# A planned attention and convolution kernel: new cost constants for the order, and 108 instead of 95 pairs of score tiles on VectorE

## The chip, the cores and the metric

The kernel runs on one core of a Trainium2 chip. A core has five engines that run side by side, each through its own instructions in a fixed order: TensorE (PE, matmuls; its weight loads are shown apart as PEld), VectorE (DVE), ScalarE (ACT), GpSimd (POOL) and SyncE (SP, which here only issues DMAs). They wait for each other through semaphores. SBUF is the on-chip memory with 128 partitions. PSUM is the memory that matmuls write, in eight banks of 512 float32 columns. The metric is the device time of a run in microseconds (us), and the median of the runs is compared.

## The reference

The inputs are a sequence x of 2048 tokens with 640 features, and k and v of the same shape. Two branches are computed and mixed by a gate for each token:

```python
x = A_q
g = _sigmoid((x * gate_w).sum(-1, keepdims=True))
a = _A_ref(x, A_k, A_v, A_shift_k, A_ssm_k, A_ssm_D)   # long convolution
b = _B_ref(x, B_wq, B_wk, B_wv, B_wo)                  # attention
return g * a + (1 - g) * b
```

Branch A shifts k with a four-tap filter, multiplies by v, convolves each feature over the sequence with ssm_k through a Fourier transform of length 4096, adds `kv * ssm_D` and multiplies by x. Branch B is attention with 32 heads of 20 features that share one key and one value head:

```python
scores = jnp.einsum("bhqd,bkd->bhqk", q, k) * (Dh ** -0.5)
p = _softmax(scores, axis=-1)
o = jnp.einsum("bhqk,bkd->bhqd", p, v)
```

There is no mask, so every head has 2048 x 2048 scores, 134 million exponentials in all.

## The kernel before

**Attention.** A score tile is 128 keys by 512 queries of one head, one PSUM bank. Four heads form a group and sit in four groups of 32 rows of TensorE's array, so that their matmuls (K = 20) can run at once. There are 32 groups G (four blocks I of 512 queries, eight groups each), with 16 key chunks j in each. The last group (LASTG = 31) is cut into three stages of 256, 128 and 128 queries, which makes its last work short. `stream` lists the tiles in order and packs them into units of three and of two tiles by turns. `QK` (L1210) writes the scores of a unit into PSUM banks 0 to 2 or 3 to 4. `EXP` (L1247) is one ScalarE instruction for a unit, from PSUM into a buffer ETA (three tiles) or ETB (two tiles); there are NET = 3 of each. `PV` (L1288) multiplies by the values with a column of ones, which gives the sum of the exponentials too, and accumulates over the 16 chunks in bank 6. The keys hold an offset that keeps the exponentials in range.

**Pairs on VectorE.** For the chunks that DVE_J names for a group, two of the four heads' tiles are left out of the stream. `DEXP` computes their exponential on VectorE: two reads of PSUM (dW, L1277, 512 wide) that scale the score into the bits of a 16-bit number, then three steps of a polynomial in the lower bits, 1024 wide (dX L1280, dX L1281, ETd L1283). There are NED = 4 buffers ETd, two dW and one dX. Their scores go to bank 5 or 7 and "ride" in row groups that a unit leaves free. Their PV matmuls use `vneg`, may only run after the first PV of the group, and must be done before its last.

**Side work.** The same engines do, between the exponentials: the query projections of the next block (L1115, L1126, sq L1130), the shift of k (L1514), the Fourier matmuls in five blocks c of 128 features and eight frequency blocks (`spectra`, L1571, with VectorE copies X L1584 and K L1590, L1592), the complex products on GpSimd (`mac`, L1604: three products of 512, one sum of 512, two of 256), the inverse transforms (`inverse`, L1637, L1647), the normalisation (`norm`: a copy of the accumulator L1356, a reciprocal, DMAs through DRAM that spread it over partitions as rbc, a GpSimd product L1368), and the output projections (`oproj` L1667 and L1670, `part` L1393 and L1396, `tail` L1423, L1447 and L1478). Side work has the PSUM banks 7 and 5 (SIDE).

**The order.** Nothing is reordered on the chip. A planner in the kernel's own source (`Scheduler`) walks through a simulated time and writes each engine's order once. Every operation has a cost (c_ps, c_fast, c_pool, c_mm, c_exp: a constant and a slope in columns) and a priority. Between engines it adds a latency (LATM, LATX). SBUF's second port, which VectorE and GpSimd share, is modelled by two times: port_until and pool_until, with the offsets PORTP and PORTD. A VectorE operation marked `port=True` starts when the last GpSimd one is done, and a GpSimd operation when the last such VectorE one is done. `pick_work` chooses for TensorE: the next operation of the main queue (score and PV matmuls in program order) when it can start, otherwise side work that fits the gap. `pick` takes the candidate of the best priority for the other engines. `emit` writes the instructions with waits on semaphores. Where TensorE would be idle, dummy matmuls (L1719) are put in. The constants change the planned order, never how long an instruction takes.

Of the kernel before, what the change touches and what calls it, by code (L numbers as in the profile page):

```python
# [23 lines left out]
LATM = {("dve", "dve"): 0.3, ("pool", "pool"): 0.0}  # L24
# [24 lines left out]
class Op:  # L49
    __slots__ = ("eng", "fn", "deps", "cost", "kind", "name", "prio", "grp", "alts", "port", "nbytes", "main",  # L50
                 "cont", "nun", "succ", "ready", "start", "end", "placed", "sig", "value", "lane", "known", "seq",
                 "banks", "last", "urge", "floating", "tail", "attached", "lat", "iss", "row", "soft", "cols", "hole", "unit")

    def __init__(self, eng, fn, cost, kind, name, prio):
        self.unit = None
        self.eng = eng
# [113 lines left out]
class Scheduler:  # L170
# [34 lines left out]
    def run(self):  # L205
# [6 lines left out]
        self.main_q = {"pe": [o for o in g.all if o.main and o.eng == "pe"],  # L212
                       "act": [o for o in g.all if o.main and o.eng == "act"]}
        self.main_pos = {"pe": 0, "act": 0}
# [43 lines left out]
    def pick(self, e, t):  # L258
# [12 lines left out]
        if e == "pool" and self.main_started and not self.pool_may(t):  # L271
            return None
        for o in self.cand[e]:
            if o.ready <= t:
# [3 lines left out]
                k = (o.prio, o.seq)  # L278
# [50 lines left out]

    def pick_work(self, t):  # L330
        q = self.main_q["pe"]
        p = self.main_pos["pe"]
        m = q[p] if p < len(q) else None
# [38 lines left out]
        if m is not None:  # L372
            if m.cont:
                if m.nun == 0:
                    self.main_pos["pe"] += 1
                    return m
                return None
            if m.nun == 0:
# [7 lines left out]
                if ok:  # L386
                    if r <= t:
                        self.main_pos["pe"] += 1
                        return m
# [60 lines left out]
    def place(self, op, e):  # L450
# [54 lines left out]
        if op.name in ("tp0", "tp1"):  # L505
# [4 lines left out]
            self.filler = self.filler2.pop(0) if self.filler2 else None  # L510
        if op.name == "pv":
            self.can_fill = not op.last
# [123 lines left out]
PORTP = 0.145  # L636
PORTD = 0.04
LASTG = 31
STAGES = ((0, 256, 6), (256, 128, 5), (384, 128, 6))
DVE_J = ((), (), (1, 6, 11), (4, 11), (2, 6, 10, 14), (4, 9, 14), (3, 8, 13), (3, 8, 11), (2, 6, 10, 14), (4, 9, 14), (1, 5, 8, 13), (2, 7, 12), (3, 8, 13), (2, 5, 8, 11, 14), (5, 12), (1, 5, 9, 13), (4, 9, 14), (4, 9, 14), (4, 9, 14), (1, 4, 8, 12), (2, 6, 10, 14), (3, 8, 13), (2, 4, 13), (1, 7, 13), (1, 6, 11), (1, 6, 11), (1, 4, 11), (3, 9), (1, 4, 7, 10, 13), (2, 5, 8, 11, 14), (2, 9), ())  # L640
MAC_ALT = ()
# [7 lines left out]
def c_fast(n):  # L649
    return 0.16 + 0.52e-3 * n  # L650

# [17 lines left out]
class Kernel:  # L669
# [256 lines left out]
    def tables2(self):  # L926
# [11 lines left out]
        for name in ("Tsin", "Tcos"):  # L938
# [7 lines left out]
            for c in range(1, H):  # L946
                self.evac(gr, "dve", lambda e, bk, name=name, c=c: e.tensor_copy(
                    T[name][:, c, 0:128 * c], self.bank_bf(bk, 128 * c, 64 * c * (c - 1))), (), [(name, c)],
                    c_fast(128 * c))
# [157 lines left out]
    def qproj(self, I, gs, prio, banks, ng):  # L1107
# [4 lines left out]
        for gl, gi in enumerate(gs):  # L1112
            gr = self.group("qp", prio, banks=banks)
            for dc in range(NDC):
# [4 lines left out]
                if dc == 0:  # L1119

                    o.deps.update(self.crow0 or ())
                    if self.crow0:
# [4 lines left out]
                          qt[:, gi, :], self.bank(bk), T["qup"][:, 0:1], None, ALU.add)), c_ps(512) + 0.055),  # L1127
# [4 lines left out]
                     [(f"qT{par}", gi)], [("sq", gl)], c_fast(512), prio=-1500.0 if I == 0 and gs[0] < 3 else prio - 500, port=True,  # L1132
# [646 lines left out]
```

## Time and profile before

| What | Before |
|---|---|
| Median of three runs | 868.13 us (867.65 to 868.68) |
| Span of the profiled execution | 865.2 us |
| Own time of the profiled execution | not listed; the median is 2.9 us above its span |
| Granted TensorE clock | 1.000 |
| First / last start of an exponential (L1247) | 19.55 / 858.17 us |
| VectorE busy in 19.5 to 125, 125 to 225, 525 to 625 us | 84.43, 88.22, 87.59 us |
| VectorE busy in 800 to 858.2 us | 25.67 us |
| Dummy matmuls L1719 in the stream | 73.84 us |

The page gives for each engine its busy time, its share of the span and its instructions. The chain is the work that ended last, followed back from the end. A group row reads: line, engine, operation, output<-input, shapes, count | busy us, mean ns of one | idle time before it, and who ended that. A timeline row reads: start, duration (a merged row: of all), engine, line, operation. A row of waits reads: engine and line waiting <- who ended it: us in total, times, longest. A row by stretch reads: stretch, its length, then busy us (and instructions) of PE, PEld, DVE, ACT, POOL, the clock, the DMA share, GB/s. Records of neighbouring instructions on ScalarE and VectorE overlap, so the distance of starts is the cost of one, not its duration.

### The profile page before, as it was taken

What the parts mean: (1) busy time and instruction counts of PE and PEld (TensorE: products, weight loads), DVE (VectorE), ACT (ScalarE), POOL (GpSimd) and SP (SyncE); (2) the same over time, 40 slices, a digit from 0 to 9 for tenths busy, and PEclk for the clock granted to TensorE, in tenths of its full rate; (3) what the DMA queues carried; (4) which work ended last, traced back from release to release, by engine and by line L of the source; (5) the groups of instructions that cost most, each with busy time, mean ns of one, the idle gap of its engine ahead of it and who ended that gap; (6) DMA issues with size and microseconds to landing.
All of it is one profiled execution on the core that took longest, in us unless ns stands there. A gap on an engine that the chain in (4) does not pass through costs nothing.

```text
span 865.2 us, 18881 instructions
## 1 busy us (share of the span) xinstructions
PE 842.1 (97%) x8139; PEld 350.5 (41%) x8159; DVE 710.2 (82%) x923; ACT 852.8 (99%) x764; POOL 389.8 (45%) x355
## 2 busy tenths in 40 slices
PE   8999999999999999999999999999999999999997
PEld 5234433344334434444434333444443444333444
DVE  8588888898999898979898988988888776688434
ACT  6999999999999999999999999999999999999997
POOL 4582000448655353665544662417677437630000
PEclk9999999999999999999999999999999999999999
DMA  7800020000100000020000021000020000041210
GB/s 197 211 14 9 20 45 20 21 14 8 44 21 20 14 20 8 20 45 20 20 15 9 19 44 49 30 14 8 20 45 20 15 14 3 13 103 39 75 60 32
DMA packets 49729, 30.71 MB, mean 35 GB/s; under 512 B 32493, under 2 KB 45678, under 8 KB 49646
## 3 DMA queue, kind: packets, MB, share of 16 engines
q1 hardware_dynamic: 49070, 29.29, 12.5%
q8 instruction: 63, 1.03, 0.5%
q10 hardware_dynamic: 576, 0.22, 0.1%
q14 instruction: 20, 0.16, 0.1%
HBM read 17.85 MB, written 6.02 MB: 28 GB/s over the span
## 4 chain that ended last, share of the span: by engine, by line
ACT 97%; PE 2%; DVE 0%; issue 0%; POOL 0%; POOLq 0%
ACT ETA L1247 58%; ACT ETB L1247 39%; PE ps L1724 1%; PE ps L1019 0%; PE ps L1051 0%; ACT xT L726 0%; PE ps L1115 0%; DVE outsb L1478 0%; DVE tprod L912 0%; POOL iota_f L865 0%; PE ps L1210 0%; PE ps L1423 0%; PE ps L1288 0%; DVE ident L873 0%; DVE acc L1409 0%
## 5 line engine op out<-in xcount | busy, mean ns | idle before, releaser
L1247 ACT ACTIVATE ETA<-ps 128x1536 bf16<-128x1536 f32 x372 | 607.2, 1632 | 0.2 <-PE ps L1210 0.2
L1247 ACT ACTIVATE ETB<-ps 128x1024 bf16<-128x1024 f32 x371 | 449.5, 1212 | 0.0
L1210 PE MATMUL ps<-qT,kT 32*128 32x512 bf16 (+2 forms) x2176 | 297.9, 371 | 12.9 <-ACT ETA L1247 7.6
L1604 POOL TENSOR_TENSOR Pp<-X,K 128x512 f32<-128x512 bf16 x120 | 164.7, 1390 | 156.5 <-DVE dX L1281 58.0
L1210 PEld LDWEIGHTS ps<-qT,kT 32*128 32x128 bf16 x2176 | 75.7, 91 | 242.2 <-ACT ETB L1247 124.2
L1277 DVE TENSOR_SCALAR dW<-ps 128x512 f32<-128x512 f32 x190 | 130.2, 685 | 42.6 <-PE ps L1210 40.7
L1288 PE MATMUL ps<-ETA,vaug 128*32 128x512 bf16 (+2 forms) x1195 | 153.1, 370 | 0.3 <-ACT ETB L1247 0.3
L1288 PE MATMUL ps<-ETB,vaug 128*32 128x512 bf16 (+2 forms) x791 | 149.7, 371 | 0.7 <-ACT ETA L1247 0.7
L1283 DVE SCALAR_TENSOR_TENSOR ETd<-dX,dW 128x1024 int16<-128x1024 f32 x95 | 134.2, 1413 | 15.4 <-PE ps L1288 15.2
L1281 DVE SCALAR_TENSOR_TENSOR dX<-dX,dW 128x1024 f32<-128x1024 f32 x95 | 133.6, 1407 | 0.2
L1280 DVE SCALAR_TENSOR_TENSOR dX<-dW 128x1024 f32<-128x1024 uint16 x95 | 131.5, 1385 | 0.9
L1604 POOL TENSOR_TENSOR AB<-Pp 128x256 bf16<-128x256 f32 x80 | 73.4, 917 | 57.7 <-DVE dX L1280 21.3
L1571 PE MATMUL ps<-ssm_kT,Tcs 128*128 128x256 bf16 x600 | 89.5, 274 | 0.0
L1637 PE MATMUL ps<-AB,Tcs 128*128 128x256 bf16 x600 | 88.4, 274 | 0.0
L1571 PE MATMUL ps<-kv,Tcs 128*128 128x256 bf16 x600 | 87.5, 275 | 0.1
L1368 POOL TENSOR_TENSOR oTn<-acc,rbc 128x512 bf16<-128x512 f32 x24 | 41.2, 1716 | 84.4 <-DMA rbc<-scr_d 37.7
L1719 PE MATMUL ps<-Tcs,zeros 128*32 128x512 bf16 (+1 forms) x920 | 74.2, 379 | 0.9 <-DVE acc L1356 0.7
L1604 POOL TENSOR_TENSOR Pp<-Pp 128x512 f32<-128x512 f32 x40 | 52.7, 1317 | 34.9 <-DVE dX L1281 10.8
L1637 PEld LDWEIGHTS ps<-AB,Tcs 128*128 128x128 bf16 x600 | 51.7, 98 | 32.6 <-issue 26.4
L1571 PEld LDWEIGHTS ps<-ssm_kT,Tcs 128*128 128x128 bf16 x600 | 50.6, 97 | 33.2 <-issue 26.3
L1571 PEld LDWEIGHTS ps<-kv,Tcs 128*128 128x128 bf16 x600 | 49.5, 98 | 35.5 <-issue 26.1
L1368 POOL TENSOR_TENSOR oT<-acc,rbc 128x512 bf16<-128x512 f32 x7 | 10.7, 1524 | 80.0 <-DMA rbc<-scr_d 47.8
(135 smaller groups left out, 645.4 us busy)
## 6 DMA issues: line engine op xcount, KB each, us to landing
rbc<-scr_d SPq DMA_DIRECT2D x31, 256.0 KB
scr_o<-oTn SPq DMA_DIRECT2D x24, 128.0 KB, 1.7
kv<-in_A_v_dram SPq DMA_DIRECT2D x4, 640.0 KB, 4.7
out_dram<-outsb SPq DMA_DIRECT2D x15, 160.0 KB, 1.9
xn<-in_A_q_dram SPq DMA_DIRECT2D x3, 640.0 KB, 6.9
oTp<-scr_o SPq DMA_DIRECT2D x12, 160.0 KB, 3.1
wog<-in_B_wo_dram SPq DMA_DIRECT2D x4, 200.0 KB
wo<-in_B_wo_dram SPq DMA_DIRECT2D x4, 200.0 KB
```

The source lines that it names most:

```text
L1210: return e.matmul(self.bank(bk, n, n * t), T["kT4"][32 * r:32 * r + 32, 128 * jt:128 * jt + 128], T[k][32 * r:32 * r + 32, g, q0:q0 + n], ...
L1247: op("act", lambda e: e.activation(et(n)[:, 0:w], self.ps[:, lo:lo + w], ACT.Exp, scale=SCALE), [("ps", base[n % 2] + k) for k in range(le ...
L1277: self.evac(gr, "dve", lambda e, bk, h=h: e.tensor_scalar(W[:, 512 * h:512 * h + 512], self.bank(bk), SCALE * LOG2E * 128.0, 128.0 * (127 ...
L1280: V(lambda e: e.scalar_tensor_tensor(X[:, :], w, DP, w, ALU.add, ALU.mult), [kW], ["dX"], c_ps(1024), **k)
L1281: V(lambda e: e.scalar_tensor_tensor(X[:, :], X[:, :], DQ, w, ALU.add, ALU.mult), [kW], ["dX"], c_ps(1024), **k)
L1283: V(lambda e: e.scalar_tensor_tensor(T[f"ETd{pe}"][:, :].bitcast(dt.int16), X[:, :], DA, W[:, :], ALU.mult, ALU.add), [kW, "dX"], [("ETd", ...
L1288: return op("pe", lambda e: e.matmul(self.bank(b, n)[32 * r:32 * r + 32, :], T[va][:, j, :], src, start=(j == 0), stop=(j == NSC - 1), til ...
L1368: self.pool(lambda e: e.tensor_tensor(out, T["acc"][:, :], T["rbc"][:, :], ALU.mult), ["acc", "rbc"], [key], c_pool(512), prio=p, port=Tru ...
L1571: self.mm(gr, lambda e, bk, lhs=lhs, rhs=rhs, comp=comp, n=n: e.matmul(self.bank(bk, 256, 256 * comp), lhs, rhs, start=(n == 0), stop=(n = ...
L1604: f = lambda e: e.tensor_tensor(out, a, b, alu)
L1637: self.mm(gr, lambda e, bk, lhs=lhs, fc=fc, comp=comp, h=h: e.matmul(self.bank(bk, 256, 256 * h), lhs, AB[:, fc, :, comp, :], start=(fc == ...
L1719: sch.filler, *sch.filler2 = ([[lambda e, r=r, st=st, b=b, n=n: e.matmul(self.bank(b, n)[32 * r:32 * r + 32, :], self.T["zeros"][:, 0:32], ...
```

## The change

- **Planner constants.** LATM gets times for each pair of engines: 0.127 between dependent VectorE operations (was 0.3), and 0.135, 0.06, 0.13 and 0.08 where 0.12 stood for all others. PORTP and PORTD change. VectorE's cost becomes c_dve and c_dve2 for the work in the stream.
- **Two main queues.** Score matmuls and PV matmuls get a queue each. `head` takes them in program order, except that scores go first when they can start and the PV batch cannot. Late PV matmuls are tied to the group's last PV batch whichever matmul of it comes first.
- **VectorE's choice.** While GpSimd is busy for over PORTW = 0.2 more, operations without the shared port go first.
- **DVE_J.** 108 pairs instead of 95, in groups 1 to 31 instead of 2 to 30, in other chunks. In group 31 a pair covers two halves of 256 queries in its first stage. A branch for steps in PSUM (INB) is there, but INB is empty.
- **mac.** The products of both parts of X with the first part of K become one of 1024; five GpSimd operations instead of six.
- **inverse.** The inverse transforms of feature block 3 come later by 90 in priority.
- **Dummy matmuls.** The set for the last stages is chosen by the PV matmul's stage.

```diff
-LATM = {("dve", "dve"): 0.3, ("pool", "pool"): 0.0}
+LATM = {("dve", "dve"): 0.127, ("pe", "dve"): 0.135, ("dve", "pe"): 0.06, ("pool", "dve"): 0.13, ("dve", "pool"): 0.08,
+        ("pool", "pool"): 0.0}
...
+        held = e == "dve" and self.main_started and self.pool_until - PORTP > t + PORTW
...
-                k = (o.prio, o.seq)
+                k = (held and o.port, o.prio, o.seq)
...
+    def startable(self, m, t):
+        if m.nun or m.ready > t:
+            return False
+        for b in m.banks or ():
+            if not self.bank_claimed[b] and (self.bank_busy[b] or self.bank_ready[b] > t):
+                return False
+        return True
+
+    def head(self, t):
+
+        a, b = ((self.main_q[x][self.main_pos[x]] if self.main_pos[x] < len(self.main_q[x]) else None) for x in ("qk", "pv"))
+        if a is None or b is None:
+            return a or b
+        if a.cont or b.cont:
+            return a if a.cont else b
+        if a.seq < b.seq:
+            return a
+        return a if not self.startable(b, t) and self.startable(a, t) else b
...
-PORTP = 0.145
-PORTD = 0.04
+PORTP = 0.05
+PORTD = 0.14
+PORTW = 0.2
+INB = ()
...
-DVE_J = ((), (), (1, 6, 11), (4, 11), (2, 6, 10, 14), (4, 9, 14), (3, 8, 13), (3, 8, 11), (2, 6, 10, 14), (4, 9, 14), (1, 5, 8, 13), (2, 7, 12), (3, 8, 13), (2, 5, 8, 11, 14), (5, 12), (1, 5, 9, 13), (4, 9, 14), (4, 9, 14), (4, 9, 14), (1, 4, 8, 12), (2, 6, 10, 14), (3, 8, 13), (2, 4, 13), (1, 7, 13), (1, 6, 11), (1, 6, 11), (1, 4, 11), (3, 9), (1, 4, 7, 10, 13), (2, 5, 8, 11, 14), (2, 9), ())
-MAC_ALT = ()
+DVE_J = ((), (2,), (4, 6, 10, 14), (2, 6, 13, 14), (1, 2, 4, 11), (7, 12, 14), (3, 10), (2, 9, 11, 12), (1, 4, 7, 10, 12, 14), (1, 9), (1, 4, 8, 10, 14), (2, 7, 12), (2, 7, 8, 13), (2, 5, 9, 13), (6, 10, 13), (1, 3, 11, 13), (), (2, 11, 14), (1, 2, 4, 9), (1, 7, 9, 13), (2, 4, 6, 10, 14), (1, 7, 10, 14), (), (2, 7, 11, 14), (5, 6, 12, 14), (3, 7, 9, 12), (3, 6, 9, 10, 12), (13,), (2, 5, 6, 14), (4, 5, 8), (1, 4, 6, 9, 11, 14), (1, 2, 4, 5))
...
+def c_dve(n):
+    return 0.065 + 1.0417e-3 * n
+
+
+def c_dve2(n):
+    return 0.07 + 0.52e-3 * n
...
-                self.inverse(c, q, base + per + 10 * q)
+                self.inverse(c, q, base + per + 10 * q + (90 if c == 3 else 0))
...
-        for o, (i, k) in enumerate(((0, 0), (1, 0), (0, 1))):
-            tt(P[:, o, :, :, :], X[:, i, :, :].unsqueeze(2).to_broadcast(sh),
-               K[:, k, :, :].unsqueeze(1).to_broadcast(sh), ALU.mult, [("X", p), ("K", p)], [("Pp", o)], 512)
+        sh2 = [128, 4, 2, CW]
+        tt(P[:, 0:2, :, :, :].rearrange("p o a k c -> p (o a) k c"),
+           X[:, :, :, :].rearrange("p i a c -> p (i a) c").unsqueeze(2).to_broadcast(sh2),
+           K[:, 0, :, :].unsqueeze(1).to_broadcast(sh2), ALU.mult, [("X", p), ("K", p)], [("Pp", 0), ("Pp", 1)], 1024)
+        tt(P[:, 2, :, :, :], X[:, 0, :, :].unsqueeze(2).to_broadcast(sh),
+           K[:, 1, :, :].unsqueeze(1).to_broadcast(sh), ALU.mult, [("X", p), ("K", p)], [("Pp", 2)], 512)
```

## The prediction

> **What bounds the kernel now.** I read the page's top first, then the chain, the costliest groups, ScalarE's timeline, the waits, and the busy time by stretch.
>
> ```profile
> span 865.2 us, 18881 instructions
> PE 842.1 (97%) x8139; PEld 350.5 (41%) x8159; DVE 710.2 (82%) x923; ACT 852.8 (99%) x764; POOL 389.8 (45%) x355
> ACT 97%; PE 2%; DVE 0%; issue 0%; POOL 0%; POOLq 0%
> L1247 ACT ACTIVATE ETA<-ps 128x1536 bf16<-128x1536 f32 x372 | 607.2, 1632 | 0.2 <-PE ps L1210 0.2
> L1247 ACT ACTIVATE ETB<-ps 128x1024 bf16<-128x1024 f32 x371 | 449.5, 1212 | 0.0
> L1277 DVE TENSOR_SCALAR dW<-ps 128x512 f32<-128x512 f32 x190 | 130.2, 685 | 42.6 <-PE ps L1210 40.7
> L1283 DVE SCALAR_TENSOR_TENSOR ETd<-dX,dW 128x1024 int16<-128x1024 f32 x95 | 134.2, 1413 | 15.4 <-PE ps L1288 15.2
> L1281 DVE SCALAR_TENSOR_TENSOR dX<-dX,dW 128x1024 f32<-128x1024 f32 x95 | 133.6, 1407 | 0.2
> L1280 DVE SCALAR_TENSOR_TENSOR dX<-dW 128x1024 f32<-128x1024 uint16 x95 | 131.5, 1385 | 0.9
> ```
>
> The chain that ended last is ScalarE for 97%: 743 exponentials in a row. TensorE is also 97% busy, but part of that is dummy work (L1719, 73.8 us inside the stream by the stretches), so it has room. The mean durations of L1247 (1632 and 1212 ns) are not what one exponential costs, since neighbours overlap in the records. The starts tell the cost:
>
> ```profile
> 399.15 1.63 ACT L1247 ACTIVATE ETA<-ps 128x1536 bf16<-128x1536 f32 x1
> 400.48 1.22 ACT L1247 ACTIVATE ETB<-ps 128x1024 bf16<-128x1024 f32 x1
> 401.39 1.66 ACT L1247 ACTIVATE ETA<-ps 128x1536 bf16<-128x1536 f32 x1
> ```
>
> A three-tile unit takes 1.33 us from start to start, a two-tile unit 0.91. The first unit starts at 19.55 and the last at 858.17. That is 838.62 us for 371 pairs of units, 2.260 us a pair. The tightest pair is about 2.23, so ScalarE loses only some 10 us in the whole stream. It is full, and only fewer tiles shorten it.
>
> **Fewer tiles on ScalarE: the whole gain.** There are 31 x 64 + 64 = 2048 score tiles. A pair on VectorE takes two of them. Before: 2048 - 190 = 1858, which is 371 pairs of units (five tiles each) and one last unit of three. After: 2048 - 216 = 1832, 366 pairs and a last unit of two. The stream loses five pairs, 5 x 2.260 = 11.3 us, and the last exponential is one tile shorter, 1.33 - 0.91 = 0.42. Together **11.7 us**.
>
> Here I weigh the Trainium skill, ScalarE: Activation LUTs, section What ACT_TABLE_LOAD costs. It gives 186 ns + 0.833 ns an element with immediate operands, and about 93 ns of overlap back to back: a repeat of 1373 and 946 ns where this trace shows 1.33 and 0.91. By the page the saving is 26 x 512 x 0.833 ns = 11.1, plus ten instructions x 93 ns = 0.9, so 12.0 us. I keep the row's 11.7.
>
> **What VectorE pays.** A pair adds two L1277, one L1280, L1281 and L1283: (130.2 + 131.5 + 133.6 + 134.2) / 95 = 5.57 us by the busy rows. Thirteen pairs are 72.5 us: 710.2 + 72.5 = 783 of about 853.5, 92% where it was 82%. That is hidden behind ScalarE as long as it comes in time. The timeline shows how much of 5.57 is the pair itself:
>
> ```profile
> 200.39 2.19 DVE L1280 SCALAR_TENSOR_TENSOR dX<-dW 128x1024 f32<-128x1024 uint16 x1
> ...
> 208.15 1.23 DVE L1280 SCALAR_TENSOR_TENSOR dX<-dW 128x1024 f32<-128x1024 uint16 x1
> 209.29 0.68 DVE L1584 TENSOR_SCALAR X<-ps 128x512 bf16<-128x512 f32 x1
> 209.89 0.68 DVE L1356 COPY acc<-ps 128x512 f32<-128x512 f32 x1
> 210.49 1.57 DVE L1281 SCALAR_TENSOR_TENSOR dX<-dX,dW 128x1024 f32<-128x1024 f32 x1
> ```
> ```profile
> 200.35 5.34 POOL L1604 TENSOR_TENSOR Pp<-X,K 128x512 f32<-128x512 bf16 x3
> ```
>
> Left alone, a 1024-wide step takes 1.14 us start to start and a 512-wide read of PSUM 0.60, so a pair is 3 x 1.14 + 2 x 0.60 = 4.6 us. Behind a GpSimd product the same step takes 2.19. The new planner constants (1.13 and 0.60 through c_dve, 0.127 between dependent steps) are near these rows. The old ones (1.225, and 0.3 more) were not, so the old plan left VectorE real slack that the new plan fills.
>
> **The merged product on GpSimd.** One 1024-wide product replaces two of 512 in each of 40 blocks. No row has that width. Alone, a 256-wide step takes 0.73 and a 512-wide one 1.15 us, so I extend the line to 1.99 (an estimate; two separate ones, 2.30, bound it above). GpSimd saves 40 x 0.31 = 12 us, at 45% load worth nothing on the path. Against it stands the Trainium skill, SBUF — State Buffer, section Who interferes with whom: VectorE instructions with two SBUF inputs contend with GpSimd's reads, and the port pair is an exclusive lock held for a whole instruction, the loser blocked. So the merged product can hold a step for 1.99 us instead of 1.15. The means (1.40 against 1.21 alone, 285 steps) put today's lock waits at about 54 us of VectorE. If steps arrive at random, they wait in proportion to the squared lengths: 40 x (1.99² + 1.15²) = 211 against 120 x 1.15² = 159, a third more on the products' part. By the lock rule that is +9 us if half the 54 is theirs. By the rows' total GpSimd time it would be slightly less than today. The new choice that takes VectorE work without the port first while GpSimd is busy lowers it. I take 0, range -20 to +9, all on VectorE and so under ScalarE.
>
> **Scores passing a waiting PV batch.** The waits of the weight loads and of VectorE:
>
> ```profile
> PEld ps L1210 <- ACT ETB L1247: 124.2, 347, 0.8
> PEld ps L1210 <- ACT ETA L1247: 105.8, 343, 0.9
> ...
> DVE ETd L1283 <- PE ps L1288: 15.2, 20, 1.8
> ...
> PEld ps L1571 <- DVE dW L1277: 3.1, 10, 0.4
> ```
>
> Score matmuls wait for ScalarE to free their banks, which is right for a full ScalarE. Waits of TensorE for VectorE are single microseconds. So passing is worth about 0 as such. It is insurance: when the last PV of a head group waits for a late pair, the next scores need not queue behind it, and six ET buffers (NET = 3 of each kind) let ScalarE run some 6 us further.
>
> **The rest.** Fewer units need 10 x 0.4 us less of score time on TensorE, and pairs ride in free row groups: nothing on the path. Inverse transforms of block 3 go behind the spectra of block 4: four groups of 32 matmuls at 88.4 / 20 = 4.4 us, 17.7 us of TensorE, covered by dummy matmuls (8.8 us at 725 to 800) and ScalarE waits. Without that cover they lengthen the end by the part not done. No DMA is added or removed. A later copy of the accumulator on VectorE delays what SP issues after it (den, rcp, rbc, the output stores), but GpSimd's normalisations (L1368) already idle 164 us before they start, and all but the last block's projections come long after. Group 31's four pairs split each score and each PV tile into two of 256 columns: as many columns, 16 matmuls more of each kind. Head: costs there are nearly the old ones, ±0.3.
>
> The tighter plan leaves VectorE a smaller lead, so some score matmuls will queue behind a TensorE instruction that waits for VectorE. No row prices this. From below 0 (or -2, if a fifth of the 10 us lost now goes). From above, a group with six pairs: 6 x 5.57 = 33 us of VectorE in 23.5 us of stream, 10 us late without a lead, and the ET buffers absorb 6, so some 4 us. I take +1, near the small waits of today.
>
> **Sum.** Against the profiled execution: 865.2 - 11.7 + 1 = 854.5 us of span. The median of the runs, 868.13, is 2.9 above the span, and the profile shows no time of its own for that run, so I carry 2.9 over: **857.4 us**.
>
> **Rivals.** (1) *VectorE starves ScalarE in the dense groups.* Six pairs stand in groups 8 and 30, five in 10, 20 and 26. For: 92% load, groups already near full. Against: four ETd buffers let it work four pairs ahead, and L1283's 15.2 us of waits for PV show that it does so today. Two or three stretches at 2 to 4 us: about 6, so 862.5 us.
>
> (2) *VectorE ends after ScalarE: slower.*
>
> ```profile
> 783.00:858.20 75.20, 74.81 (x854) 32.30 (x851) 40.54 (x68) 75.20 (x68) 4.60 (x3) 1.00 0.16 52
> ```
>
> In the last 75 us VectorE is busy 40.5 us, 15.9 of them with pairs (its four lines in that stretch), so 24.7 with the rest. Afterwards groups 29 to 31 hold 13 pairs, 72.4 us: 97 in 75 us. Four pairs ahead take off 22.3 us and it just fits. Each pair not made ahead moves the output projections 5.57 us past the stream, and from 2.1 pairs (11.7 us) the kernel is slower. With three missing: 857.4 + 16.7 = 874 us. Against it: at 4.6 us a pair 12 us are spare.
>
> (3) *The change does nothing measurable:* ScalarE has fewer tiles and waits as much longer, 867 us. Nothing in the waits supports it.
>
> **Chances.** Likeliest 0.66 (own range 855 to 860); rival 1 0.20; rival 3 0.04; rival 2 0.10. Below 855: 0.04; above 864.5: rivals 2 and 3 and the tail of 1, some 0.16. A measurement of this kernel tells about 0.2%, 1.7 us, from no change: faster 0.86, same 0.04, slower 0.10.
>
> **What would show it.** Right: 367 three-tile-buffer and 366 two-tile-buffer exponentials, starts 1.33 and 0.91 apart in all stretches, the last start near 847, 7 us or less behind it; VectorE near 90%. Wrong: starts spread in stretches where L1210 or L1288 waits for VectorE; VectorE busy with L1670 or L1396 after the last exponential; L1604's wide product well over 2 us.

## The result, and the profile after

The changed kernel takes 864.72 us (median of four runs, 864.12 to 866.22). The kernel before took 868.40 in the same comparison. The ratio is 0.996, with a 95% interval from 0.9946 to 0.9974. The change is faster by 3.7 us, where 10.7 were forecast. The time lies above the forecast's own range of 855 to 860 us, and just above 864.5, a region to which it gave a chance of 0.16.

The page of the changed kernel: its span, the engines, and the chain of work that ended last. In this kernel the lines have moved: scores are L1243 (were L1210), exponentials L1280 (L1247), dW L1313 (L1277), the three steps of a pair L1325, L1326 and L1328 (L1280, L1281, L1283), PV L1333 (L1288), spectra L1622 (L1571), inverse L1690 (L1637), products L1655 (L1604), dummy matmuls L1772 (L1719).

```profile
span 864.4 us, 18503 instructions
...
PE 840.7 (97%) x7963; PEld 350.2 (41%) x7963; DVE 782.3 (90%) x987; ACT 845.7 (98%) x755; POOL 375.7 (43%) x315
...
ACT 45%; PE 27%; DVE 24%; issue 2%; POOL 1%; POOLq 0%; DVEq 0%
...
L1280 ACT ACTIVATE ETA<-ps 128x1536 bf16<-128x1536 f32 (+1 forms) x367 | 566.6, 1544 | 6.0 <-PE ps L1243 5.3
L1280 ACT ACTIVATE ETB<-ps 128x1024 bf16<-128x1024 f32 x366 | 411.2, 1123 | 0.2 <-PE ps L1243 0.2
...
L1313 DVE TENSOR_SCALAR dW<-ps 128x512 f32<-128x512 f32 x216 | 147.0, 681 | 26.2 <-PE ps L1243 25.7
L1328 DVE SCALAR_TENSOR_TENSOR ETd<-dX,dW 128x1024 int16<-128x1024 f32 x108 | 158.5, 1467 | 3.0 <-PE ps L1333 2.7
...
L1326 DVE SCALAR_TENSOR_TENSOR dX<-dX,dW 128x1024 f32<-128x1024 f32 x108 | 154.1, 1427 | 0.7
...
L1325 DVE SCALAR_TENSOR_TENSOR dX<-dW 128x1024 f32<-128x1024 uint16 x108 | 151.5, 1403 | 1.3
```

ScalarE has its 367 and 366 exponentials and is busy for 98%, nearly as before. The chain tells the change: it was ScalarE for 97%, and now it runs through TensorE and VectorE for half of the time. That is what a stream with small waits everywhere looks like. The idle time of L1280, 6 us, shows only part of it, because records of neighbouring exponentials overlap, so that a late one first loses its overlap. The starts show all of it. I call the **excess** what the distances of the starts have over 1.330 us (behind a three-tile unit) and 0.903 us (behind a two-tile unit), summed over the stream:

| Profiled execution | Before | After | Difference |
|---|---|---|---|
| first start of an exponential | 19.55 | 20.46 | +0.91 |
| stream without excess | 828.4 | 817.3 | -11.2 |
| excess | 10.2 | 20.0 | +9.9 |
| last start to the end | 7.03 | 6.63 | -0.40 |
| span | 865.2 | 864.4 | -0.8 |

The two profiled executions are not typical ones. The changed kernel's is the longest of its four (866.22 us, 1.8 over its span; the spans of the four go from 862.3 to 864.4), and no span on record for the kernel before is shorter than 865.2 us (median 866.1). A part of the difference is the granted TensorE clock. By stretch, after:

```profile
703.50:706.90 3.40, 2.48 (x28) 0.67 (x22) 3.40 (x6) 3.40 (x4) 2.16 (x3) 1.00 0.00 0
706.90:710.30 3.40, 3.40 (x21) 1.04 (x22) 2.63 (x3) 2.49 (x3) 0.94 (x2) 0.50 0.02 2
```

For 3.4 us the clock was 0.50, and in and right behind this stretch ScalarE lost 1.8 of the 20.0 us. Before, the clock was 1.000 through the whole stream. So at the full clock the excess is 18.3 us, 8.1 more than before. The two runs of the changed kernel with a clock of 1.000 have spans of 862.3 and 862.4. Whether TensorE's waits bring such a drop about isn't shown.

Before, 15 starts came more than 0.1 us late, 2.3 us in all. After, 48 do, 14.2 us in all (three of them, 1.8 us, at the half clock), and they lie in all parts of the stream: between 0.2 and 2.3 us of excess in every 50 us. Of the 20.0 us, 16.6 lie behind two-tile units, where the next scores are those of a unit of three. One of the 48 by the timeline (start, duration, engine, line, operation; in brackets idle time and who ended it):

```profile
486.26 2.06 DVE L1326 SCALAR_TENSOR_TENSOR dX<-dX,dW 128x1024 f32<-128x1024 f32 x1
...
487.24 1.68 ACT L1280 ACTIVATE ETA<-ps 128x1536 bf16<-128x1536 f32 x1
...
487.63 0.39 PE L1243 MATMUL ps<-qT,kT 32*128 32x512 bf16 x2 [0.16 <-ACT ETB L1280]
488.24 0.68 DVE L1313 TENSOR_SCALAR dW<-ps 128x512 f32<-128x512 f32 x1
488.59 1.25 ACT L1280 ACTIVATE ETB<-ps 128x1024 bf16<-128x1024 f32 x1
...
488.98 0.38 PE L1243 MATMUL ps<-qT,kT 32*128 32x512 bf16 x1 [0.96 <-DVE dW L1313]
...
489.29 1.05 PE L1772 MATMUL ps<-Tcs,zeros 128*32 128x512 bf16 x16
...
490.27 0.39 PE L1243 MATMUL ps<-qT,kT 32*128 32x512 bf16 x3
...
490.76 1.45 ACT L1280 ACTIVATE ETA<-ps 128x1536 bf16<-128x1536 f32 x1 [0.92 <-PE ps L1243]
```

VectorE's step L1326 took 2.06 us instead of the 1.2 of an undisturbed one, so its read of a score bank (L1313) came at 488.24. TensorE's next score, one of a pair, needs that bank and starts at 488.98. Behind it in TensorE's fixed order stand 16 dummy matmuls and only then the scores of the next unit, at 490.27. ScalarE starts 2.17 us after its last start instead of 0.90. In 34 of the 48 cases (11.2 of the 14.2 us) TensorE or its weight loads waited for VectorE between 1.5 us ahead of the previous start and the late one; at the starts that are in time this holds for 36%. Dummy matmuls stand behind that wait in eight of the 34 (2.9 us).

The waits of the changed kernel (engine and line waiting <- who ended it: us, times, longest) show how common that is:

```profile
PEld ps L1622 <- DVE dW L1313: 9.4, 22, 1.0
...
ACT ETA L1280 <- PE ps L1243: 5.3, 13, 0.9
...
PEld ps L1243 <- DVE dW L1313: 4.4, 8, 1.3
```

The first was 3.1 us, the second and third 0.2 us each before. All waits of TensorE and its weight loads for VectorE sum to 60.5 us, where they were 26.9.

### The profile page after: what moved, and what is told of

The parts are those of the page before. It is cut to its first block, busy times and chain, and to the rows that moved or that the text cites. A ratio compares the mean times of both kernels' runs of the same rounds, so it can differ in the third digit from the quotient of the medians.

```text
span 864.4 us, 18503 instructions
## 1 busy us (share of the span) xinstructions
PE 840.7 (97%) x7963; PEld 350.2 (41%) x7963; DVE 782.3 (90%) x987; ACT 845.7 (98%) x755; POOL 375.7 (43%) x315
## 3 DMA queue, kind: packets, MB, share of 16 engines
q1 hardware_dynamic: 49070, 29.29, 12.5%
## 4 chain that ended last, share of the span: by engine, by line
ACT 45%; PE 27%; DVE 24%; issue 2%; POOL 1%; POOLq 0%; DVEq 0%
ACT ETA L1280 27%; ACT ETB L1280 18%; PE ps L1243 8%; DVE dX L1326 6%; DVE ETd L1328 5%; DVE dX L1325 4%; PE ps L1333 4%; PE ps L1622 4%; DVE dW L1313 4%; PE ps L1690 3%; PE ps L1772 2%; PE ps L1720 2%; DVE qT L1159 1%; DVE X L1635 1%; PE ps L1777 1%
## 5 line engine op out<-in xcount | busy, mean ns | idle before, releaser
L1280 ACT ACTIVATE ETA<-ps 128x1536 bf16<-128x1536 f32 (+1 forms) x367 | 566.6, 1544 | 6.0 <-PE ps L1243 5.3
L1280 ACT ACTIVATE ETB<-ps 128x1024 bf16<-128x1024 f32 x366 | 411.2, 1123 | 0.2 <-PE ps L1243 0.2
L1243 PE MATMUL ps<-qT,kT 32*128 32x512 bf16 (+2 forms) x2176 | 304.1, 372 | 10.4 <-ACT ETA L1280 2.8
L1655 POOL TENSOR_TENSOR Pp<-X,K 128x1024 f32<-128x1024 bf16 (+1 forms) x80 | 150.7, 1896 | 130.1 <-DVE K L1643 62.9
L1243 PEld LDWEIGHTS ps<-qT,kT 32*128 32x128 bf16 x2176 | 78.1, 91 | 234.3 <-ACT ETB L1280 102.4
L1313 DVE TENSOR_SCALAR dW<-ps 128x512 f32<-128x512 f32 x216 | 147.0, 681 | 26.2 <-PE ps L1243 25.7
L1328 DVE SCALAR_TENSOR_TENSOR ETd<-dX,dW 128x1024 int16<-128x1024 f32 x108 | 158.5, 1467 | 3.0 <-PE ps L1333 2.7
L1326 DVE SCALAR_TENSOR_TENSOR dX<-dX,dW 128x1024 f32<-128x1024 f32 x108 | 154.1, 1427 | 0.7
L1333 PE MATMUL ps<-ETA,vaug 128*32 128x512 bf16 (+2 forms) x1174 | 154.1, 372 | 0.1
L1325 DVE SCALAR_TENSOR_TENSOR dX<-dW 128x1024 f32<-128x1024 uint16 x108 | 151.5, 1403 | 1.3
L1333 PE MATMUL ps<-ETB,vaug 128*32 128x512 bf16 (+2 forms) x778 | 148.1, 373 | 0.2 <-ACT ETA L1280 0.2
L1655 POOL TENSOR_TENSOR AB<-Pp 128x256 bf16<-128x256 f32 x80 | 71.7, 896 | 72.7 <-DVE dX L1326 26.6
L1622 PE MATMUL ps<-ssm_kT,Tcs 128*128 128x256 bf16 x600 | 89.8, 274 | 2.5 <-DVE dW L1313 2.0
L1690 PE MATMUL ps<-AB,Tcs 128*128 128x256 bf16 x600 | 89.7, 276 | 0.3 <-DVE dW L1313 0.2
L1622 PE MATMUL ps<-kv,Tcs 128*128 128x256 bf16 x600 | 87.1, 275 | 0.7 <-DVE dW L1313 0.4
L1419 POOL TENSOR_TENSOR oTn<-acc,rbc 128x512 bf16<-128x512 f32 x24 | 38.8, 1616 | 85.6 <-DMA rbc<-scr_d 67.3
L1655 POOL TENSOR_TENSOR Pp<-Pp 128x512 f32<-128x512 f32 x40 | 53.7, 1342 | 42.3 <-DVE dX L1325 12.9
L1622 PEld LDWEIGHTS ps<-ssm_kT,Tcs 128*128 128x128 bf16 x600 | 50.6, 98 | 38.5 <-issue 26.8
L1690 PEld LDWEIGHTS ps<-AB,Tcs 128*128 128x128 bf16 x600 | 51.6, 98 | 34.2 <-issue 25.7
L1622 PEld LDWEIGHTS ps<-kv,Tcs 128*128 128x128 bf16 x600 | 49.8, 98 | 35.1 <-issue 24.0
L1772 PE MATMUL ps<-Tcs,zeros 128*32 128x512 bf16 (+1 forms) x724 | 61.5, 383 | 0.4 <-DVE acc L1407 0.3
L1419 POOL TENSOR_TENSOR oT<-acc,rbc 128x512 bf16<-128x512 f32 x7 | 10.1, 1449 | 108.3 <-DMA rbc<-scr_d 58.1
```

Source lines behind the costliest of these rows:

```text
L1243: return e.matmul(self.bank(bk, n, n * t), T["kT4"][32 * r:32 * r + 32, 128 * jt:128 * jt + 128], T[k][32 * r:32 * r + 32, g, q0:q0 + n], ...
L1280: op("act", lambda e: e.activation(et(n)[:, 0:w], self.ps[:, lo:lo + w], ACT.Exp, scale=SCALE), [("ps", base[n % 2] + k) for k in range(le ...
L1313: self.evac(gr, "dve", lambda e, bk, c=c: e.tensor_scalar(W[:, c], self.bank(bk), SCALE * LOG2E * 128.0, 128.0 * (127 - KDN) - 32768.0, AL ...
L1325: V(lambda e: e.scalar_tensor_tensor(X[:, :], w, DP, w, ALU.add, ALU.mult), [kW], ["dX"], c_dve(1024), **k)
L1326: V(lambda e: e.scalar_tensor_tensor(X[:, :], X[:, :], DQ, w, ALU.add, ALU.mult), [kW], ["dX"], c_dve(1024), **k)
L1328: V(lambda e: e.scalar_tensor_tensor(E, X[:, :], DA, W[:, :], ALU.mult, ALU.add), [kW, "dX"], [("ETd", pe)], c_dve(1024), **k)
```

## The experiments

The question is why TensorE waits so much for VectorE. Candidates: VectorE has too much to do (90% where it was 82%); the merged product holds the port; the passing of PV batches disturbs the order; or the new planner constants leave an order in which VectorE has no reserve, which is time that the plan gives to an operation beyond what the chip needs. A kernel's numbers are in one table; the sections tell what each says. "Waits" are those of TensorE and its weight loads for VectorE. The last column is the part of the excess in and right behind stretches of the stream in which the granted clock was 0.50.

| Kernel | Time, us | Ratio to before, 95% | VectorE busy | Waits, us | Excess, us | Of it at half clock, us |
|---|---|---|---|---|---|---|
| before | 867.9 to 868.4 | | 710.2 | 26.9 | 10.2 | 0 |
| after | 864.72 | 0.9946 to 0.9974 | 782.3 | 60.5 | 20.0 | 1.8 |
| short_steps | 857.32 | 0.9862 to 0.9891 | 753.3 | 34 | 11.7 | 0 |
| split_product | 864.16 | 0.9941 to 0.9971 | 775.6 | 58.8 | 17.5 | 0 |
| no_passing | 865.78 | 0.9960 to 0.9982 | 784.2 | 58.9 | 18.8 | 0 |
| old_pairs | 879.22 | 1.0111 to 1.0145 | 727.7 | 60.1 | 21.2 | 3.5 |
| short_products | 859.83 | 0.9890 to 0.9919 | 769.9 | 44.3 | 13.5 | 0 |
| short_reads | 861.00 | 0.9903 to 0.9936 | 770.6 | 45.6 | 14.2 | 0 |
| old_pairs_old_constants | 869.58 | 1.0012 to 1.0025 | 729.8 | 36.7 | 11.8 | 0 |
| old_pairs_old_cost | 873.26 | 1.0044 to 1.0071 | 723.0 | 34.3 | 10.0 | 0 |
| old_pairs_old_latency | 876.97 | 1.0084 to 1.0111 | 732.2 | 51.4 | 20.3 | 3.4 |
| reserve_104_pairs | 861.36 | 0.9909 to 0.9937 | 765.8 | 37.8 | 11.6 | 0 |
| some_reserve_108_pairs | 889.54 | 1.0224 to 1.0258 | 796.8 | 58.1 | 37.3 | 0 |
| reserve_108_pairs | 906.72 | 1.0416 to 1.0463 | 792.4 | 47.1 | 61.4 | 3.0 |

**short_steps: the same order, faster steps.** The planned order of every engine stays; only two of VectorE's steps get shorter, by computing 896 of 1024 columns.

```diff
-V(lambda e: e.scalar_tensor_tensor(X[:, :], w, DP, w, ALU.add, ALU.mult), ...)
-V(lambda e: e.scalar_tensor_tensor(X[:, :], X[:, :], DQ, w, ALU.add, ALU.mult), ...)
+V(lambda e: e.scalar_tensor_tensor(X[:, 0:896], w[:, 0:896], DP, w[:, 0:896], ALU.add, ALU.mult), ...)
+V(lambda e: e.scalar_tensor_tensor(X[:, 0:896], X[:, 0:896], DQ, w[:, 0:896], ALU.add, ALU.mult), ...)
```

> The order of the changed kernel, instruction for instruction; the first two polynomial steps of each pair on VectorE work on 896 columns instead of 1024 (the last 128 columns of each pair are wrong; one memset more at the start). That takes 216 x 0.133 = 28.8 us off VectorE (90% to about 87%). Theory A (VectorE arrives later than the plan has it, TensorE waits for it in front of the next scores): most of the extra 9.9 us of ScalarE waits go, 856 to 859 us. Rival B (the order itself, scores and PV exchanged or the side work, delays TensorE whatever VectorE does): 863 to 865 us.

Its page and its wait of ScalarE for scores:

```profile
span 855.3 us, 18487 instructions
...
ACT 88%; PE 10%; DVE 2%; issue 0%
```
```profile
ACT ETA L1280 <- PE ps L1243: 0.9, 3, 0.4
```

VectorE is busy for 29.0 us less and the kernel is 7.4 us faster. The excess falls from 20.0 to 11.7, near that of before, and the chain is ScalarE's again. So ScalarE's new waits hang on VectorE being late: TensorE's order is the same here, and costs little when VectorE comes in time. At 857.32 it runs at the forecast time, with an excess 1.5 us above that of before, where +1 was forecast. It isn't a kernel to be had, since it leaves out an eighth of two steps.

**split_product: the merged product as two.** The planned order stays; the 1024-wide product is issued as two of 512 in one planned operation.

```diff
-tt(P[:, 0:2, :, :, :].rearrange("p o a k c -> p (o a) k c"),
-   X[:, :, :, :].rearrange("p i a c -> p (i a) c").unsqueeze(2).to_broadcast(sh2),
-   K[:, 0, :, :].unsqueeze(1).to_broadcast(sh2), ALU.mult, [("X", p), ("K", p)], [("Pp", 0), ("Pp", 1)], 1024)
+def two(e):
+    for o in range(2):
+        r = e.tensor_tensor(P[:, o, :, :, :], X[:, o, :, :].unsqueeze(2).to_broadcast(sh),
+                            K[:, 0, :, :].unsqueeze(1).to_broadcast(sh), ALU.mult)
+    return r
+
+self.pool(two, [("X", p), ("K", p)], [("Pp", 0), ("Pp", 1)], c_pool(1024), prio=prio, port=True, name="mac")
```

> The order of the changed kernel; where GpSimd has one product of 1024 it issues two of 512 one after the other (40 instructions more, the result is the same). Theory C (the long lock of the merged product makes VectorE late): VectorE's longest steps fall from 3.0 to 2.2 us and 3 to 6 us come back, 859 to 862 us. Theory A, in which the total load counts: within 1.5 us of the changed kernel, 863 to 866 us, a little slower if GpSimd's extra 12 us lock VectorE more.

0.9941 to 0.9971 against the changed kernel's 0.9946 to 0.9974: no difference. VectorE is busy for 6.7 us less and its longest step falls from 3.0 to 2.3 us, so the merged product does hold its steps longer, but the waits stay at 58.8 us and the excess at 17.5, against 18.3 at the full clock. It is not the cause.

**no_passing: PV batches in program order.** `head` no longer lets scores pass.

```diff
-        return a if not self.startable(b, t) and self.startable(a, t) else b
+        return b
```

> The changed kernel with the main queue in program order (scores never pass a PV batch), planned anew; 54 lines of TensorE's order differ. If passing works as insurance on the chip, taking it away costs 1 to 4 us (866 to 869 us). If it is worth nothing, within 1 us of the changed kernel. If passing itself delays scores (rival B), 1 to 4 us faster.

865.78: about 1 us slower than the changed kernel, with overlapping intervals, and with nearly the same waits. Passing is neither the gain nor the trouble.

**old_pairs: the new planner with the 95 old pairs.** Only the list differs from the changed kernel (shortened here).

```diff
-DVE_J = ((), (2,), (4, 6, 10, 14), (2, 6, 13, 14), (1, 2, 4, 11), ...)
+DVE_J = ((), (), (1, 6, 11), (4, 11), (2, 6, 10, 14), ...)
```

> The changed kernel with the old list of 95 pairs, planned anew. Its stream is as long as before. If the new planner constants alone cost the waits (theory D: latencies planned too short), TensorE waits for VectorE as often as in the changed kernel and the time is 5 to 10 us above the kernel before: 873 to 878 us. Theory A (too little reserve at 108 pairs): the waits stay near the old 10 us, 866 to 870 us.

```profile
span 877.2 us, 18889 instructions
...
PE 847.4 (97%) x8169; PEld 354.7 (40%) x8187; DVE 727.7 (83%) x922; ACT 857.5 (98%) x765; POOL 370.9 (42%) x315
...
ACT 57%; PE 29%; DVE 12%; issue 1%; POOL 0%; POOLq 0%
```

This was the surprise. With the pairs of the kernel before, VectorE is at 83%, and yet the waits are 60.1 us, the excess is 21.2, and the kernel is 11 us slower than before. Of the excess 3.5 us lie at the half clock (all four runs have a clock of 0.994 to 0.996), which leaves 17.7, as much as in the changed kernel. So the idea that 108 pairs are too much load fell. Something in the rest of the change makes VectorE late even at the old load.

**short_products and short_reads: whose lateness?** Again the planned order of the changed kernel stays. In one, GpSimd's products and sum take 112 of 128 columns (the first block apart). In the other, VectorE's reads of score banks take 432 of 512 columns, an operation that doesn't use the shared port (in the changed kernel 39 of these reads lie wholly beside GpSimd work and repeat every 0.60 to 0.61 us, like those beside an idle GpSimd, while steps of a pair take up to 3.0).

```diff
+w = CW if c == 0 and fc == 0 else 112
+n = slice(0, w)
...
-   K[:, 0, :, :].unsqueeze(1).to_broadcast(sh2), ALU.mult, [("X", p), ("K", p)], [("Pp", 0), ("Pp", 1)], 1024)
+   K[:, 0, :, n].unsqueeze(1).to_broadcast(sh2), ALU.mult, [("X", p), ("K", p)], [("Pp", 0), ("Pp", 1)], 1024)
...
```
```diff
-self.evac(gr, "dve", lambda e, bk, c=c: e.tensor_scalar(
-    W[:, c], self.bank(bk), SCALE * LOG2E * 128.0,
+self.evac(gr, "dve", lambda e, bk, c=slice(512 * h, 512 * h + (512 if self.ndexp < 3 else 432)): e.tensor_scalar(
+    W[:, c], self.bank(bk, c.stop - c.start), SCALE * LOG2E * 128.0,
```

> The order of the changed kernel; GpSimd's two products and its sum use 112 of 128 columns of each part in all blocks but the first (their last columns are stale, so the convolution is wrong). That takes 39 x (0.21 + 0.11 + 0.11) = 17 us off GpSimd and nothing off VectorE. Theory E (the plan lets GpSimd start about 0.085 us too early after VectorE, and the merged product takes 2.12 us where the plan has 2.02: GpSimd holds the shared port later than planned, VectorE slips, TensorE waits): most of the 9.9 us come back, 857 to 860 us. If VectorE's own load makes the lateness: at most 2 us come back, 863 to 866 us.

> The order of the changed kernel; VectorE's reads of scores from PSUM (L1313) take 432 instead of 512 columns in all pairs but the first two (stale numbers in the rest of the pair). That takes 212 x 0.083 = 17.7 us off VectorE, as much as the other run takes off GpSimd, in instructions that do not use the shared port. If only the port makes VectorE late (theory E in its strict form): 861 to 864 us. If any reserve on VectorE will do (theory A): 857 to 860 us.

Both help: 4.9 us for VectorE's busy time 12.4 us less, and 3.7 us for 11.7 less. With short_steps (7.4 for 29.0) that is 0.26 to 0.40 us of time for each us of VectorE's. No one of these kinds of operation holds the lateness: each that gets shorter helps. But the busy time alone doesn't price it, since split_product took 6.7 us off VectorE for only 0.6. At 861.00 short_reads ends at the edge between its two forecasts, so it doesn't tell how large the port's part is.

**old_pairs with the old constants, all or some.** The next three start from old_pairs, with VectorE at the same load. First the old latencies, the old port offsets and the old cost of a VectorE operation. (A few costs of single operations, such as the normalisation's product, keep their new values.)

```diff
-LATM = {("dve", "dve"): 0.127, ("pe", "dve"): 0.135, ("dve", "pe"): 0.06, ("pool", "dve"): 0.13, ("dve", "pool"): 0.08,
-        ("pool", "pool"): 0.0}
+LATM = {("dve", "dve"): 0.3, ("pool", "pool"): 0.0}
-PORTP = 0.05
-PORTD = 0.14
+PORTP = 0.145
+PORTD = 0.04
...
-    return 0.065 + 1.0417e-3 * n
+    return 0.16 + 1.04e-3 * n
```

> The changed kernel with the 95 old pairs and also the old planner constants (latencies, port offsets, 0.16 instead of 0.065 in VectorE's cost), planned anew; merged product, passing and VectorE's choice stay. Against the run with 95 pairs and the new constants (879.2 us) only the constants differ. Theory D/E (the new constants leave no reserve): the waits return to about 10 us and the time to 866 to 870 us. If the merged product or the new choices make the waits: 874 us or more.

869.58: with these constants the time is 9.6 us shorter, of which 5.9 are excess at the full clock (11.8 instead of 17.7) and the rest is mostly the half clock, which doesn't occur here. The rest of the change without the new pairs is about where the kernel before was (+0.2%). Then only the cost (the last two lines of that diff), and only LATM (its first three):

> The run with 95 old pairs and the new constants (879.2 us), but VectorE's planned cost is 0.16 us + 1.04 ns a column again instead of 0.065 us + 1.0417 ns: one line, planned anew. That is 0.095 us of reserve on each of some 900 VectorE operations. Theory F (this reserve kept TensorE from waiting): the extra 11 us of ScalarE waits go, 866 to 872 us (the plan itself ends a few us later). If the latencies make the waits: 876 us or more.

> The run with 95 old pairs and the new constants (879.2 us), but with the old latencies between engines (0.3 between dependent VectorE operations, 0.12 elsewhere), planned anew; VectorE's cost stays at the new 0.065. Theory F: the waits stay, 874 to 881 us. If the short latencies make the waits: 866 to 871 us.

The waits of ScalarE for scores and of TensorE for VectorE, in old_pairs_old_cost and then in old_pairs_old_latency (one line less ahead of the same code there):

```profile
PEld ps L1622 <- DVE dW L1313: 3.1, 10, 0.5
...
ACT ETA L1280 <- PE ps L1243: 0.2, 1, 0.2
```
```profile
PEld ps L1621 <- DVE dW L1312: 5.7, 14, 0.9
...
ACT ETA L1279 <- PE ps L1242: 5.0, 12, 1.1
...
PEld ps L1242 <- DVE dW L1312: 4.5, 9, 1.6
```

With the old cost the excess is 10.0, as before the change; with the old latencies it is 16.9 at the full clock, near the 17.7 of old_pairs. Each constant makes the planner write another order, but the three agree: it is the 0.095 us by which the old cost of each VectorE operation lay above its repeat in the traces (0.692 against 0.60 for a read of 512) that kept TensorE from waiting. (The order with the old cost gains less time than that, 873.26, and misses its range of 866 to 872: its end is longer, 12.0 us behind the last exponential's start instead of 6.9. The planner planned it so, with 12.5.)

The planner's own times say the same. It is plain Python in each kernel's source, and run without the chip it gives the length of the stream that it planned, from the first to the last start of an exponential. Planned and measured are 838.7 and 838.6 us before, 827.5 and 837.3 after, 838.7 and 849.7 in old_pairs, 838.7 and 848.7 with the old latencies, and 838.7 and 838.4 with the old cost. None of these five plans has more than 0.1 us of waits of ScalarE. So the old pairs fit the new planner as well as the old one, and it is the chip that falls behind the plan, by more than the half clock's part. (The plan's c_exp, 0.0633 us and 0.8333 ns a column, counts each exponential 13 ns longer than its undisturbed repeat. That is 10 us in a stream, so an excess of 10 us is the plan's own pace.)

**The reserve with 108 pairs, whole and in part.** The changed kernel with nothing but the cost changed, to 0.16 + 1.04e-3 n and to 0.10 + 1.0417e-3 n:

```diff
-    return 0.065 + 1.0417e-3 * n
+    return 0.16 + 1.04e-3 * n
```

> The changed kernel with its 108 pairs, and only the planned cost of a VectorE operation put back to 0.16 + 1.04e-3 n (0.095 us more for each). It asks whether the reserve alone mends the changed kernel. If the reserve is all that is missing, the waits of TensorE for VectorE fall to about 35 us, ScalarE loses about 10 us in the stream instead of 20, and the time is about 855. If the 108 pairs, in these chunks, have no room for the reserve (108 pairs with five operations each, and the reserve on each, are 51 us of VectorE's planned time more), the planner itself spreads the exponentials: ScalarE loses 25 us or more, with waits that come in few long pieces in the groups with five and six pairs, and the time is above 870.

> The changed kernel with 108 pairs and about a third of the reserve: the planned cost of a VectorE operation is 0.10 + 1.0417e-3 n, 0.035 us more than in the changed kernel. If the reserve is all that is missing, some of the 10 us of new waits go: about 860 to 863. If these pairs leave no room for it, the time lies above 864.7, between the changed kernel and the one with the whole reserve.

Both are far slower than before: the first case of the expectation failed, the second came true in the main. The longest wait of ScalarE in reserve_108_pairs, by its waits and by its timeline:

```profile
ACT ETB L1280 <- PE ps L1333: 31.0, 4, 24.5
```
```profile
283.21 3.02 DVE L1328 SCALAR_TENSOR_TENSOR ETd<-dX,dW 128x1024 int16<-128x1024 f32 x1
...
286.29 0.39 PE L1333 MATMUL ps<-ETd,vneg 128*32 128x512 bf16 x2 [1.56 <-DVE ETd L1328]
...
286.78 1.02 ACT L1280 ACTIVATE ETB<-ps 128x1024 bf16<-128x1024 f32 x1 [24.52 <-PE ps L1333]
```

Here a head group's last PV waits for its last pair on VectorE (ETd), and ScalarE for an ET buffer that PV has to free. The planner, which takes VectorE to be slower, writes an order in which the pairs of some groups come too late. It knew it: its own plan already has 44.4 us of waits of ScalarE, 22.7 of them at this place (and 20.4 with a third of the reserve). On the chip there are ten gaps of over 1 us, with 51.3 us of excess. The first two, 2.6 us, lie at the half clock. The other eight come behind the ends of the groups 8 and 10 to 15 and of group 31's first stage, so behind groups with three and four pairs too, and not only with five and six as expected. In the rest of the stream at the full clock the excess is 9.6. Counting the same way (gaps of up to 1 us at the full clock) it is 14.4 with a third of the reserve and 17.0 without any; with the 95 pairs it is 10.0 with the reserve and 16.7 without. So the small waits go as the reserve grows, with either list of pairs; but the list of 108 has no room for the reserve.

**reserve_104_pairs: faster than before and after.** Part of the reserve goes where the traces show time that the plan lacks (below), with a list of 104 pairs that fits it:

```diff
-        ("dve", "pe"): 0.06, ("dve", "act"): 0.06, ("dve", "dve"): 0.0, ("dve", "pool"): 0.08, ("act", "act"): 0.1,
+        ("dve", "pe"): 0.12, ("dve", "act"): 0.06, ("dve", "dve"): 0.0, ("dve", "pool"): 0.15, ("act", "act"): 0.1,
-LATX = 0.12
+LATX = 0.14
-LATM = {... ("dve", "pe"): 0.06, ("pool", "dve"): 0.13, ("dve", "pool"): 0.08,
+LATM = {... ("dve", "pe"): 0.14, ("pool", "dve"): 0.13, ("dve", "pool"): 0.165,
+                d = self.order["dve"]
+                if self.main_started and HOLD and len(d) > 1 and d[-1].end > t and not d[-1].port:
+                    start = max(start, d[-2].end + LATM["dve", "pool"])
-PORTD = 0.14
+PORTD = 0.056
-    return 0.065 + 1.0417e-3 * n
+    return 0.07 + 1.0417e-3 * n
...
-                    ALU.mult, ALU.add), ["omgf", ("A", i)], [("outsb", i % 4)], c_dve(HD))
+                    ALU.mult, ALU.add), ["omgf", ("A", i)], [("outsb", i % 4)], 0.458)
```

(The merged product is planned at 2.1 us, `part` and the last projections at 0.458 too.)

> A version that tries to beat both: the changed kernel with 104 pairs in other chunks, and a plan nearer to what the traces show: VectorE to TensorE 0.14 (was 0.06) and 0.14 for a freed bank, VectorE to GpSimd 0.165 (was 0.08), also where GpSimd waits for the VectorE operation before the last; PORTD 0.056; the merged product 2.1; the output projection's read 0.458; VectorE's cost 0.070. The stream has 1840 tiles, 3.5 us more than with 108 pairs. Theory A/F: extra ScalarE waits fall from 9.9 to 1 to 3 us, 859 to 862 us. If the plan's accuracy doesn't matter: 866 to 868 us.

```profile
span 858.9 us, 18568 instructions
...
PE 836.2 (97%) x8004; PEld 350.2 (41%) x8004; DVE 765.8 (89%) x967; ACT 846.3 (99%) x758; POOL 363.0 (42%) x315
...
ACT 90%; PE 8%; DVE 2%; issue 0%; POOL 0%; POOLq 0%
```

861.36 us: four pairs fewer put eight tiles more on ScalarE, 8 x 0.447 = 3.6 us (2.233 for five tiles), and the excess of 11.6 instead of 18.3 at the full clock gives back more. VectorE is busy for 89%, one point less than in the changed kernel, and the waits fell from 60.5 to 37.8 us. Several constants changed at once here, so this run shows a better trade, not which of them made it.

## Why the prediction was wrong

**Fewer tiles, -11.7: right.** Five pairs of units less are 11.2 us of the stream at the undisturbed repeats, and 0.4 at the end is the last exponential's missing tile: 11.6. By the rule of the Trainium skill's page (ScalarE: Activation LUTs, section What ACT_TABLE_LOAD costs) the estimate was 12.0 and by the trace's repeats 11.7, which was nearer.

**VectorE's 783 us: right in size, wrong in what followed.** It is 782.3. A pair costs (147.0 + 151.5 + 154.1 + 158.5) / 108 = 5.66 us by the rows, where 5.57 was taken. "Hidden as long as it comes in time" was the right condition, but the text then asked only whether VectorE has enough time in a group or at the end. It came late at single banks, and kept TensorE waiting for up to 1.3 us at a time.

**The merged product, 0 on the path: right.** Alone it takes 2.12 us, not 1.99. The text named "well over 2 us" as a bad sign; it came true, and yet splitting the product changed nothing.

**Passing, about 0: right** (no_passing).

**Head and rest: ±0.3** was too narrow for one execution. The head was +0.9, but in the five profiled kernels with the same planned order (after, short_steps, split_product, short_products, short_reads) the first start lies anywhere from 19.65 to 21.19 us, so this isn't shown to be the change's. The last stages were right: the end is 6.6 us behind the last start. The 16 more matmuls of each kind for group 31 were wrong, without effect: there are 2176 score matmuls in both kernels.

**The term that failed: "+1" for the tighter plan, with a range of -2 to +4.** It measured +9.9 us in the profiled executions: +8.1 at the full clock, and 1.8 at the half clock, for which the forecast had no term. The medians agree: -3.7 in all, less the -11.6 of the tiles, leaves +7.9 for this term and the head. The text said itself that the old plan left VectorE real slack and that the new plan fills it, and then priced that from the waits of before, "near the small waits of today". Those waits were small because of the slack. old_pairs_old_cost shows it with the load unchanged: a cost constant that is 0.095 us higher takes the excess at the full clock from 17.7 to 10.0. The upper bound, six pairs in a group less what the ET buffers hold, thought of a backlog; the waits that came are short, everywhere, and in a stall like the one shown no ET buffer helps, because TensorE's fixed order puts the next scores behind the late bank.

**Rival 1** (VectorE starves ScalarE, 862.5) had the right engine and nearly the size, but the wrong place: not in dense groups. **Rival 2** (VectorE ends after ScalarE) and **rival 3** (nothing) were not seen. Against rival 2 the text counted 12 us to spare at 4.6 us a pair; nine pairs (four being made ahead) and 24.7 us of other work in 75.2 leave 9.

**The 2.9 us around the span** were two things: 1.8 in most runs, and so, it seems, a profiled execution about 1 us quicker than the median. Forecast and result are both medians, so this moves no part of their difference of 7 us; it does widen the difference of the two profiled executions.

What is left open: which of the planner's times are too short, and by how much each matters. The traces show some candidates. From the start of a 512-wide VectorE read to TensorE's matmul in the freed bank it takes 0.735 us, of which 0.60 is the repeat, so 0.135 are the latency, where LATM has 0.06. GpSimd starts 79 ns after the recorded end of a VectorE instruction (median), and that end lies 84 ns behind the point where VectorE's next one may start, which is the end that c_dve counts: 0.163 in the planner's terms, where it has 0.08. A projection's read repeats at 0.46 where c_dve(320) is 0.398. That each is a cause is argued, not shown. Nor was it tried what the dummy matmuls add, which in the stall shown stood between the late score and the next unit's, or whether the half-clock stretches follow from TensorE's waits.

## What to carry to other kernels

In an order that is planned ahead, a cost that is "too high" can be the reserve that covers what the plan doesn't know; making it true removes the reserve, and a change that does so must be charged for it. The waits of the kernel before can't price that, because they were measured with the reserve in place; shortening one kind of instruction under an unchanged order can, and so can the old constant under the old load. The planned length of the stream beside the measured one shows the lateness at once (827.5 against 837.3 us). And the busy share doesn't tell it: 83% busy was as late as 90%, and 89% with a part of the reserve was nearly in time.

## What the hardware showed that I had not expected

- Merging two 512-wide GpSimd products into one of 1024 saves little: 2.12 us alone, against 2 x 1.15.
- GpSimd, waiting for VectorE's instruction, starts 79 ns after its recorded end, so a chain that goes between the two engines loses this at each turn.
- The time of a run is mostly 1.75 to 2.1 us above its own span, whatever the order; single runs of the kernel before show up to 3.3.
- The granted TensorE clock fell to 0.50 in mid-stream, for 3.4 us in the changed kernel (1.8 us lost) and for 13.7 us in old_pairs_old_latency (3.4 us lost by ScalarE).
